# A planned attention and MLP kernel: fillers ahead of the products with v, and the broadcast of inverted sums as a step of its own

## The chip, the cores and the metric

The kernel runs on one core of a Trainium2 chip. A core has TensorE (PE, matrix products), ScalarE (ACT, here the exponentials and tanh), VectorE (DVE, elementwise work), GpSimd (POOL) and SyncE (SP, which issues most of the DMAs). They run side by side and wait for each other through semaphores; each takes its own instructions strictly in order. The metric is the time of one execution in microseconds (us); the time of a kernel is the median of its runs.

## The reference

Two branches are computed from the same x (2048 rows of 640 features) and mixed by a gate:

```
g = sigmoid((x * gate_w).sum(-1))
qkv = x @ wqkv;  32 heads of 20 features
p = softmax(q k^T / sqrt(20));  a = (p v) @ wo
h = x @ w1 + b1  (1536 features)
b = (h * tanh(softplus(h))) @ w2
out = g * a + (1 - g) * b
```

All inputs and the output are bf16. The exponentials of the scores, 32 x 2048 x 2048 of them, are the largest part of the elementwise work.

## The kernel before, in words

**Tiles.** The 32 heads form 8 groups of 4, the 2048 queries form 4 chunks of 512. A score tile is 128 keys by 512 queries of one head; there are 2048 of them. They are kept transposed (keys on the partitions). The first chunks, 0 and 1, are taken group by group, and the projections of q, k and v are made in between; chunks 2 and 3 follow.

**Slots.** The work is cut into 683 slots of three score tiles. In a slot PE makes the three products (`score_mms`, matmul at L1055) into three PSUM banks, ACT takes one exponential over them (L1077, in `emit_e`, PSUM to the buffer ETS, five slots deep), and PE later multiplies the tiles with v (`pv`, L1180), four heads side by side, into one PSUM bank, ACC. v carries a column of ones, so the same product also gives the softmax's sums. Banks 0 to 5 hold the scores of two slots in turn, 6 is ACC, and 7 is for everything else.

**Units.** In some slots the third tile isn't given to ACT: DVE computes its exponential by a polynomial in four operations, and that tile is called a unit. `emit_x` does the first, L1094, which reads the scores from PSUM; the others, L1110 twice and L1112, follow in two lanes. `choose` decides before each slot whether it gets a unit; before it is asked, the loop over slots tests that the work behind its due time is under CATCH_UP, that the lag of tasks is under LAG or little DVE work is queued, and that DVE has room until the end. CHAIN is a reserve in `choose` for the time that a unit needs before its group of heads ends.

**Fillers.** All other matrix work is a list of tasks with due slots: projections (L538, L590, L684, L711), the gate's and the safety test's parts, w1 (`h_task`, L845), w2 (`b_task`, L906) and the output product with wo (L930). A task is some matmuls into bank 7 and a `finish`, which lets DVE drain the bank (for w1 at L855, adding the bias); the next task may begin when the drain is done. `pick` takes the next task that fits into the slot, `put` issues one of its matmuls. What a slot owes to the fillers is counted in `owed`; `now["open"]` is a task that was begun and not ended. A forced task that is due is issued whole, whether it fits or not.

**The plan.** The program is written by a planner that runs when the kernel is built. `Plan.add` appends an instruction to its engine, with assumed costs, and keeps a clock for each engine (`pl.now`); the order in which instructions are added is the order in which each engine takes them. The assumed times only choose the order; on the chip the waits on semaphores decide. `dve` puts an operation on DVE, and before it such queued pieces of DVE work as end within SLACK of the time at which its input is ready (LATER in place of SLACK for drains of fillers when little is owed). `work` picks those pieces from several queues: `norm` first, then the lanes of units, the pieces of the activation (`blend`) and background work.

**Sums.** When a group of heads has had its last product with v, `group_done` copies ACC to OUNG (L1258), and SP moves the sums to RR in a compact form (L1261). The rest stands in the queue `norm`: `invert` takes the reciprocals (L1265), SP writes them to a DRAM buffer SUMS (L1266) and reads them back broadcast over the partitions into BCT (L1268, 256 KB), and `times` multiplies (L1226). OUNG and BCT are held until then. SP adds L1266 and L1268 one right after the other.

**w1 blocks.** `load_w1` (L801, on SP, 320 KB each) loads 48 blocks in turn into two buffers. A block is loaded when the matmuls of the task that used the same buffer have read it; `h_task`'s `finish` adds the load. Their home is the tile W2R for the first 12, then REG.

Of the kernel before, what the change touches and what calls it, by code (L numbers as in the profile page):

```python
# [45 lines left out]
HOP = 0.1  # L46
TAIL = {"pe": 0.17, "act": 0.12, "dve": 0.125, "pool": 0.1, "sp": 2.0}
SWITCH = 0.1
COL = 1 / 2400.0
PASS = CW * COL  # L50
EXP = 1.335
# [3 lines left out]
WIDE = 0.60  # L55
# [2 lines left out]
LANES = 2  # L58
TAKEN = 3.3
SLACK = 0.3  # L60
LATER = 0.9
FREE = 0.2
RISK = {"pe": 0.1, "act": 0.3, "dve": 0.5, "pool": 1.2, "sp": 0.6}
CHAIN = 3.0
AHEAD = 14
BEHIND = 7.0
PATIENCE = 3.0
CATCH_UP = 4.0
BUSY = 0.6
CROWD = 1.4  # L70
MARGIN = 0.5
# [4 lines left out]
LAST = 0  # L76
END = 45
SHIFT = 0.4
LAG = 12
SPARE = 3.5  # L80
WINDOW = 3.41
CALM = 4
# [5 lines left out]
H_AT = 150  # L88
H_STEP = 12.5
THIN = 0.09  # L90
CUTS = ((0, 256), (256, 256))


# [122 lines left out]
def bass_gated_mix__softmax_full_mha__dense_activation_mish__prompt_kernel(  # L216
# [42 lines left out]
    RR = sb("RR", [P, 16], FP32)  # L259
# [12 lines left out]
    SUMS = nc.dram_tensor("SUMS", [HG, CW], FP32, kind="Internal")  # L272
# [54 lines left out]
    NSLOT = -(-NC * NG * NKT * HG // SLOT)  # L327
# [5 lines left out]
    def attention(pl, fast):  # L333
# [4 lines left out]
        tasks = []  # L338
# [3 lines left out]
        norm = deque()  # L342
# [113 lines left out]
        if fast:  # L456
# [328 lines left out]
                return Task([mm(f) for f in range(NFT)], w * COL, finish, due,  # L785
                            lambda: [*sq_ops[n], m_one] if len(sq_ops.get(n, ())) == NFT else None)

            w1_load, w1_last = {}, {}
            w2_load = []

            def load_w1(n):

                k = n % 6
                if n < 2:
                    deps = []
                elif n in (FIRST, FIRST + 1):
                    assert len(sq_ops) >= 4
                    deps = list(wkv_read)
                else:
                    deps = [w1_last[n - 2]]  # L800
                w1_load[n] = pl.add("sp", lambda e: e.dma_start(  # L801
                    w1b(n), B_w1[:, k * HW:(k + 1) * HW].rearrange("(f p) c -> p f c", p=P)),
                    deps, f"w1{n % 2}", cost=0.75, tail=1.7, bulk=1.5)

            def load_w2():
                w2_load.append(pl.add("sp", lambda e: e.dma_start(
# [403 lines left out]
        oung_free, rr_read, bc_read = [None], [None], [None]  # L1210
# [3 lines left out]
        def group_done(c, g, step, last):  # L1214


            end = c == NC - 1 and g >= NG - 1

            def reads():
                if fast:  # L1220
                    return [low_last[0]] if c >= 2 else [zeros, *turned, *(k_moved if g >= 6 else ())]
                assert c < 2 or g > 0 or len(otn_read[c % 2]) == 8
                return otn_read[c % 2]

            def times(src, deps):
                oung_free[0] = bc_read[0] = otn_done[(c, g)] = pl.add("dve", lambda e: e.tensor_tensor(  # L1226
                    otn(c, g, fast), src, BC, ALU.mult), [*deps, *reads()], cost=WIDE)
                if g == NG - 1:
                    otn_read[c % 2] = []

            if end:
                while norm:
                    norm.popleft()[1]()
                if (c, g) == groups[-1]:
                    flush(lambda: not any(soon))
                for at, w in ([cut[(c, g)]] if fast else [(n * HW, HW) for n in range(2)]):
                    cols = slice(at, at + w)
                    src, bc, rr = PS[:, ACC, cols], BC[:, cols], RR[:, at // 32:(at + w) // 32]
                    cost = w * COL * 2.6 + 0.09
                    if (c, g) != groups[-1]:  # L1240
                        held = OUNG[:, cols]
                        last = acc_free[0] = pl.add(
                            "dve", lambda e, src=src: e.tensor_copy(held, src), [last, oung_free[0]], cost=cost)
                        src = held
                    a = pl.add("dve", lambda e, src=src, bc=bc: e.transpose(bc, src), [last, bc_read[0]], cost=cost)
                    a = pl.add("dve", lambda e, bc=bc, rr=rr, w=w: e.reciprocal(rr, bc[:, 0:w:32]), [a, rr_read[0]], cost=0.15)
                    a = pl.add("dve", lambda e, bc=bc, rr=rr, w=w: e.transpose(
                        bc.rearrange("p (a r) -> p a r", r=32), rr.unsqueeze(2).to_broadcast([P, w // 32, 32])),
                        [a], cost=cost)
                    to = otn(c, NG - 1, fast)[:, cols]  # L1250
                    end_done.append(pl.add("dve", lambda e, src=src, bc=bc, to=to: e.tensor_tensor(
                        to, src, bc, ALU.mult), [a, *reads()], cost=cost))
                oung_free[0] = bc_read[0] = rr_read[0] = otn_done[(c, g)] = end_done[-1]
                return
            while oung_free[0] == "busy":
                norm.popleft()[1]()
            src = OUNG[:, :]
            ev = dve(lambda e: e.tensor_copy(src, PS[:, ACC, :]), [last, oung_free[0]], WIDE)  # L1258
            oung_free[0] = "busy"
            acc_free[0] = ev  # L1260
            got = pl.add("sp", lambda e: e.dma_start(  # L1261
                RR[:, :], OUNG[0:P:32, :].rearrange("j (r a) -> j r a", a=16)), [ev, rr_read[0]], "nr0", cost=0.55, tail=1.4)

            def invert():
                r = pl.add("dve", lambda e: e.reciprocal(RR[:, :], RR[:, :]), [got], cost=0.25)  # L1265
                rr_read[0] = pl.add("sp", lambda e: e.dma_start(  # L1266
                    SUMS.ap().rearrange("j (r a) -> (j r) a", a=16), RR[:, :]), [r, *spread_last], "nr1", cost=0.4, tail=1.7)
                spread_last[:] = [pl.add("sp", lambda e: e.dma_start(  # L1268
                    BC, SUMS.ap().unsqueeze(1).to_broadcast([HG, 32, CW])),
                    [rr_read[0], bc_read[0]], "nr2", cost=0.55, tail=4.7)]  # L1270
                spread = list(spread_last)
                norm.append((WIDE, lambda: times(src, spread), lambda: spread[-1]))
            norm.append((0.25, invert, lambda: got))


# [179 lines left out]
        for step in range(NSLOT + 40):  # L1455
            now["step"] = step
            if step >= NSLOT and not queue and not tasks and not any(k >= step for k in at):
                break

            for t in [t for t in tasks if t.forced and t.due <= step]:  # L1460
                while now["open"] not in (None, t):
                    put(now["open"])
                while t in tasks:
                    put(t)
            if step < NSLOT:
                emit_e(step)
            if fast and area[0] and not w2_load and len(h_done) >= FIRST and all(ei_free[(0, b)] != "busy" for b in range(3)):
                load_w2()
            if fast and step == SQ - 18:
                squares(0)  # L1470
                squares(1)
            if acts and safe(acts[0][0]) < pl.now["act"] and mish_free():
                acts.popleft()[1]()
            ahead = able = 0.0
            rate = behind = 0.0
            lag = max((step - t.due for t in tasks if not t.forced and t.ready() is None), default=0)
            for t in tasks:
                slack = max(1, t.due - AHEAD * t.forced - step)
                ahead += t.left()
                rate = max(rate, ahead / slack)  # L1480
                if t.forced or t is now["open"] or t.ready() is not None:
                    able += t.left()
                    behind = max(behind, able / slack)
            now["rate"] = rate
            if step + 2 < NSLOT:
                compose(step + 2, choose(step + 2) if fast and step >= CALM and (step < slot_of(0, 1, 0) or behind < CATCH_UP and (lag < LAG or backlog() < SPARE) and room()) else None)
                emit_s(step + 2)
                to_come = pv_ready() * PASS
                if owed + rate > 0.1 and pick(pl.now["pe"] + 0.8):
                    to_come += min(owed + rate, 0.4)  # L1490
                fill_up(to_come, False)

                if fast and step + 2 in off:
                    emit_x(step + 2)
            emit_pv(step, 2 if step < NSLOT - 1 else 99)

            limit = pl.now["act"] + EXP + HOP if step < NSLOT else 1e9
            owed = min(owed + rate, 1.0) if step < NSLOT else 1e9
            while owed > 0:
                t = pick(limit)  # L1500
                if t is None:
                    break
                put(t)
                owed -= t.cost
            fill_up(0.0, True)
            for fn in at.pop(step, []):
                fn()
            work(pl.now["act"] + 0.5 if step < NSLOT else 1e9)
# [168 lines left out]
```

## Time and profile before

| | |
|---|---|
| median of 3 runs | 880.14 us (878.48 to 881.72) |
| profiled execution | 881.69 us, span 879.9 us |
| busy | ACT 858.4 us (98%), DVE 818.7 (93%), PE 744.8 (85%), POOL 15.4 (2%) |
| exponentials (L1077) | 683, of which 203 over two tiles |
| DMA | 42.44 MB, 48 GB/s over the span |

The span goes from the first to the last instruction; the time of an execution includes a little around it. In rows of groups, the numbers are the line, engine and operation, what is written and read, the count, then the busy time in us and the mean duration of one in ns, then the idle time of that engine just ahead of these instructions and what ended it. A row of waits reads "who <- for whom: us in total, times, longest". A row of the chain is a start, a length and what carried the chain then; a row of the record in order of time is a start, a length, engine, line and operation, with the idle time ahead of it in brackets. SPq rows are DMA issues of SP. A row of stretches is from:to, length, busy time with the count of instructions, the granted clock of TensorE, the share of the DMA engines and GB/s.

### The profile page before, as it was taken

How to read it: one execution, taken by the hardware profiler on the slowest of the kernel's cores; microseconds unless marked ns; L12 is line 12 of the kernel's file. 1: busy time of each engine (PE TensorE's matmuls, PEld its weight loads, DVE VectorE, ACT ScalarE, POOL GpSimd, SP SyncE). 2: the span in 40 equal slices, each digit the busy share in tenths (PEclk: the TensorE clock that was granted, in tenths of full speed). 3: DMA queues.
4: the chain of work that ended last, by engine and by line, in shares of the span. 5: the costliest groups of instructions: out<-in, count | busy, mean ns of one | idle time of the engine just before them, and what ended most of it. 6: DMA issues, size and time to landing. Idle time of an engine off the chain costs nothing.

```text
span 879.9 us, 15312 instructions
## 1 busy us (share of the span) xinstructions
PE 744.8 (85%) x6249; PEld 259.3 (29%) x6291; DVE 818.7 (93%) x1421; ACT 858.4 (98%) x714; POOL 15.4 (2%) x29
## 2 busy tenths in 40 slices
PE   8888888888878888888888888898888788998885
PEld 3232232222322233223223233333333233332222
DVE  5899999999588998999999999999999799999996
ACT  6999999999999999999999999999999799999996
POOL 2000000000000000000000000000000000000000
PEclk9999999999999999999999999999999899999999
DMA  9112110011122110131121121111211212010001
GB/s 215 28 50 60 56 32 13 8 49 37 41 60 63 57 57 28 44 100 37 41 64 42 54 74 31 46 32 40 69 48 43 72 34 71 21 32 18 14 14 35
DMA packets 69870, 42.44 MB, mean 48 GB/s; under 512 B 20472, under 2 KB 65776, under 8 KB 69744
## 3 DMA queue, kind: packets, MB, share of 16 engines
q1 hardware_dynamic: 67424, 40.89, 16.5%
q8 instruction: 52, 0.85, 0.4%
q10 hardware_dynamic: 2256, 0.47, 0.3%
q0 software_dynamic: 112, 0.01, 0.1%
q14 instruction: 26, 0.21, 0.1%
HBM read 33.97 MB, written 5.23 MB: 45 GB/s over the span
## 4 chain that ended last, share of the span: by engine, by line
ACT 95%; PE 2%; DMA 1%; DVE 1%; issue 0%; ACTq 0%
ACT ETS L1077 93%; ACT REG L877 2%; DMA REG<-in_B_w_dram 1%; ACT W2R L877 1%; PE PS L1055 1%; PE PS L490 1%; PE PS L845 0%; DVE HB L936 0%; PE PS L1436 0%; PE PS L649 0%; PE PS L658 0%; PE PS L1180 0%; PE PS L769 0%; PE PS L930 0%; DVE HB L855 0%
## 5 line engine op out<-in xcount | busy, mean ns | idle before, releaser
L1077 ACT ACTIVATE ETS<-PS 128x1536 bf16<-128x1536 f32 (+1 forms) x683 | 837.9, 1479 | 6.2 <-PE PS L1055 6.1
L1055 PE MATMUL PS<-QT,KT 32*128 32x512 bf16 (+1 forms) x2267 | 281.7, 379 | 114.7 <-ACT ETS L1077 102.9
L1180 PE MATMUL PS<-ETS,V_all 128*21 128x512 bf16 (+1 forms) x1901 | 211.5, 380 | 0.3 <-ACT ETS L1077 0.3
L1055 PEld LDWEIGHTS PS<-QT,KT 32*128 32x128 bf16 x2267 | 69.3, 91 | 324.9 <-ACT ETS L1077 302.6
L1180 PEld LDWEIGHTS PS<-ETS,V_all 128*21 128x21 bf16 x1901 | 48.6, 89 | 93.4 <-issue 89.1
L906 PE MATMUL PS<-W2R,HB 128*128 128x320 bf16 x384 | 71.6, 302 | 0.9 <-DVE OUTT L936 0.6
L1110 DVE SCALAR_TENSOR_TENSOR EM<-EM 128x512 f32<-128x512 f32 x101 | 68.9, 682 | 0.1
L1110 DVE SCALAR_TENSOR_TENSOR ER<-ER 128x512 f32<-128x512 f32 x101 | 68.7, 680 | 0.0
L1094 DVE TENSOR_SCALAR XE<-PS 128x512 f32<-128x512 f32 x80 | 54.7, 686 | 8.3 <-PE PS L1055 7.2
L845 PE MATMUL PS<-XB,REG 128*128 128x256 bf16 x360 | 55.2, 279 | 3.7 <-DMA REG<-in_B_w_dram 3.4
L1094 DVE TENSOR_SCALAR REG<-PS 128x512 f32<-128x512 f32 x74 | 50.7, 686 | 2.2 <-PE PS L1055 1.8
L538 PE MATMUL PS<-XB,WOQ 128*128 128x512 bf16 x135 | 42.2, 384 | 2.7 <-issue 2.4
L906 PEld LDWEIGHTS PS<-W2R,HB 128*128 128x128 bf16 x384 | 30.0, 97 | 36.7 <-issue 24.4
L855 DVE TENSOR_TENSOR HB<-PS,B1F 128x512 bf16<-128x512 f32 x48 | 32.9, 685 | 6.0 <-PE PS L845 5.8
L845 PEld LDWEIGHTS PS<-XB,REG 128*128 128x128 bf16 x360 | 29.9, 98 | 28.7 <-issue 22.3
L1094 DVE TENSOR_SCALAR W2R<-PS 128x512 f32<-128x512 f32 x48 | 32.9, 686 | 3.1 <-PE PS L1055 2.4
L896 DVE SCALAR_TENSOR_TENSOR U<-U,HB 128x512 f32<-128x512 f32 x48 | 32.8, 683 | 0.0
L895 DVE SCALAR_TENSOR_TENSOR U<-U 128x512 f32<-128x512 f32 x48 | 32.7, 680 | 0.0
L550 DVE CAST QT<-PS 128x512 bf16<-128x512 f32 x31 | 21.3, 687 | 7.2 <-PE PS L538 6.8
L1110 DVE SCALAR_TENSOR_TENSOR ER<-XE 128x512 f32<-128x512 uint16 x40 | 27.4, 685 | 0.2
L1110 DVE SCALAR_TENSOR_TENSOR EM<-XE 128x512 f32<-128x512 uint16 x40 | 27.3, 683 | 0.2
L1112 DVE SCALAR_TENSOR_TENSOR XE<-ER,XE 128x512 int32<-128x512 f32 x40 | 27.4, 684 | 0.1
(115 smaller groups left out, 797.3 us busy)
## 6 DMA issues: line engine op xcount, KB each, us to landing
REG<-in_B_w_dram SPq DMA_DIRECT2D x36, 320.0 KB, 3.2
BCT<-SUMS SPq DMA_DIRECT2D x31, 256.0 KB
W2R<-in_B_w_dram SPq DMA_DIRECT2D x12, 320.0 KB, 3.2
KT<-KS SPq DMA_DIRECT2D x28, 128.0 KB
KS<-OTN SPq DMA_DIRECT2D x16, 128.0 KB, 1.8
W2R<-in_B_w_dram SPq DMA_DIRECT2D x1, 1920.0 KB, 9.4
out_dram<-OUTT SPq DMA_DIRECT2D x24, 80.0 KB, 1.6
REG<-in_A_wqkv_dram SPq DMA_DIRECT2D x2, 700.0 KB, 8.2
```

What stands on the lines that cost most here:

```text
L538: return lambda e, bank: e.matmul(PS[:, bank, :], pads[:, b, f, :], xt(c)[:, f, :], start=(f == 0), stop=(f == NFT - 1))
L845: return lambda e, bank: e.matmul(PS[:, bank, i * HW:(i + 1) * HW], w1b(n1)[:, f, i * P:(i + 1) * P], xt(c)[:, f, cols], start=(f == 0), s ...
L855: ev = dve(lambda e: e.tensor_tensor(hb, PS[:, bank, :].rearrange("p (i t) -> p i t", i=2), bias, ALU.add), [last, *b1f, *sq_read.values() ...
L895: piece(WIDE, lambda e: e.scalar_tensor_tensor(U2[:, :], U2[:, :], EVEN[0], U2[:, :], ALU.add, ALU.mult))
L896: piece(WIDE, lambda e, to=to: e.scalar_tensor_tensor(U2[:, :], U2[:, :], EVEN[1], to, ALU.add, ALU.mult))
L906: return lambda e, bank: e.matmul(PS[:, bank, 0:HALF], HB[:, hc % 2, f, t * P:(t + 1) * P], W2[:, f, half * HALF:(half + 1) * HALF], start ...
L1055: op = pl.add("pe", lambda e, i=i, g=real(g), tile=tile, j=j, cols=cols, c=c, of_q=of_q: e.matmul(scores(s)[:, i, cols], KT[32 * j:32 * j ...
L1077: e_op[s] = pl.add("act", lambda e: e.activation(ETS[:, s % NETS, 0:n, :], scores(s)[:, 0:n, :], AF.Exp, scale=SCALE, bias=LIFT if fast el ...
L1094: ev_op[s] = dve(lambda e: e.tensor_scalar(y, scores(s)[:, 2, :], SCALE * ULPS, BIAS, ALU.mult, ALU.add), [s_op[s], ei_free[b], *(wkv_read ...
L1110: piece(WIDE, lambda e, v=m if i else f, i=i: e.scalar_tensor_tensor(m, v, STEPS[i], v, ALU.add, ALU.mult), lambda i=i: () if i else [lane ...
L1112: piece(WIDE, lambda e: e.scalar_tensor_tensor(x, m, LAST_STEP, y, ALU.mult, ALU.add))
L1180: lasts[n] = pl.add("pe", lambda e, tile=tile, h=real(g) * HG + j, j=j, src=src[:, cols], of_q=of_q, count=count: e.matmul(PS[32 * j:32 * ...
```

## The change

Four things change, beside parameters of the planner.

In a slot, the rest of a task that is open is issued ahead of the products with v if all of it is at most what is owed plus OVER (0.2 us), and fits before the slot's end with one pass and one switch to spare. Before, fillers came after the products with v in each slot. `emit_pv` itself is not changed.

The spreading of inverted sums, L1268, leaves `invert` and becomes a function `spread`, which is put into the queue `norm` and is taken when the planner holds the write of SUMS to be done. That write is assumed to land 2.8 us after its issue instead of 1.7.

A w1 load also depends on the load before it into the same buffer.

The parameters: LATER 0.9 to 0.5, CHAIN 3.0 to 3.3, CATCH_UP 4.0 to 5.0, LAG 12 to 9. With all of it the plan has 207 units.

```diff
-LATER = 0.9
+LATER = 0.5
-CHAIN = 3.0
+CHAIN = 3.3
-CATCH_UP = 4.0
+CATCH_UP = 5.0
-LAG = 12
+LAG = 9
+OVER = 0.2
...
-            w1_load, w1_last = {}, {}
+            w1_load, w1_last, w1_newest = {}, {}, {}
...
+                deps = [*deps, w1_newest.get(n % 2)]
                 w1_load[n] = pl.add("sp", lambda e: e.dma_start(
                     w1b(n), B_w1[:, k * HW:(k + 1) * HW].rearrange("(f p) c -> p f c", p=P)),
                     deps, f"w1{n % 2}", cost=0.75, tail=1.7, bulk=1.5)
+                w1_newest[n % 2] = w1_load[n]
...
                 rr_read[0] = pl.add("sp", lambda e: e.dma_start(
-                    SUMS.ap().rearrange("j (r a) -> (j r) a", a=16), RR[:, :]), [r, *spread_last], "nr1", cost=0.4, tail=1.7)
+                    SUMS.ap().rearrange("j (r a) -> (j r) a", a=16), RR[:, :]), [r, *spread_last], "nr1", cost=0.4, tail=2.8)
+                norm.append((0.0, spread, lambda: rr_read[0]))
+
+            def spread():
                 spread_last[:] = [pl.add("sp", lambda e: e.dma_start(
                     BC, SUMS.ap().unsqueeze(1).to_broadcast([HG, 32, CW])),
                     [rr_read[0], bc_read[0]], "nr2", cost=0.55, tail=4.7)]
-                spread = list(spread_last)
-                norm.append((WIDE, lambda: times(src, spread), lambda: spread[-1]))
+                wide = list(spread_last)
+                norm.append((WIDE, lambda: times(src, wide), lambda: wide[-1]))
...
-            emit_pv(step, 2 if step < NSLOT - 1 else 99)
-
             limit = pl.now["act"] + EXP + HOP if step < NSLOT else 1e9
             owed = min(owed + rate, 1.0) if step < NSLOT else 1e9
+            if fast and step < NSLOT and now["open"] and now["open"].left() <= min(owed + OVER, limit - pl.now["pe"] - PASS - SWITCH):
+                t = now["open"]
+                while t in tasks:
+                    put(t)
+                    owed -= t.cost
+            emit_pv(step, 2 if step < NSLOT - 1 else 99)
+
             while owed > 0:
```

## The prediction

> **What bounds the kernel now.** I read the page of the profile first: the span, the busy shares and the chain that ended last.
>
> ```profile
> span 879.9 us, 15312 instructions
> PE 744.8 (85%) x6249; PEld 259.3 (29%) x6291; DVE 818.7 (93%) x1421; ACT 858.4 (98%) x714; POOL 15.4 (2%) x29
> ACT 95%; PE 2%; DMA 1%; DVE 1%; issue 0%; ACTq 0%
> ```
>
> ScalarE (ACT) is busy 98% of the span and carries 95% of the chain, so the time is the sum of ACT's exponentials, plus the places where ACT stands idle, plus a start and an end. Second view: ACT's groups by line and shape, and what ACT waited for.
>
> ```profile
> L1077 ACT ACTIVATE ETS<-PS 128x1536 bf16<-128x1536 f32 x480 | 682.4, 1601 | 5.4 <-PE PS L1055 5.4
> L1077 ACT ACTIVATE ETS<-PS 128x1024 bf16<-128x1024 f32 x203 | 225.9, 1191 | 0.8 <-PE PS L1055 0.6
> ACT ETS L1077 <- PE PS L1055: 6.1, 5, 3.8
> ```
>
> A slot is one exponential of three score tiles (480 times) or of two (203 times); in the latter the third tile is a unit that VectorE (DVE) computes. The last slot has two tiles anyway, since 2048 tiles are 682 slots of three and one of two, so 202 units run now. Between first and last exponential ACT waited 6.1 us in five places, 3.8 us of it in one. Third view, the chain at that place (a transfer on it), and the record in order of time around it:
>
> ```profile
> 686.49 7.22 DMA REG<-in_B_w_dram
> ```
>
> ```profile
> 684.42 0.50 PE L845 MATMUL PS<-XB,REG 128*128 128x256 bf16 x3
> ...
> 682.71 0.34 SPq L1266 DMA_DIRECT2D SUMS<-RR  x1
> 685.92 0.53 SPq L1268 DMA_DIRECT2D BCT<-SUMS  x1
> 686.49 11.17 SPq L801 DMA_DIRECT2D REG<-in_B_w_dram  x3
> ...
> 688.45 0.69 DVE L855 TENSOR_TENSOR HB<-PS,B1F 128x512 bf16<-128x512 f32 x1
> ...
> 693.76 1.25 PE L845 MATMUL PS<-XB,REG 128*128 128x256 bf16 x5 [3.42 <-DMA REG<-in_B_w_dram]
> ...
> 695.59 1.45 ACT L1077 ACTIVATE ETS<-PS 128x1536 bf16<-128x1536 f32 x1 [3.76 <-PE PS L1055]
> ...
> 697.85 2.36 ACT L1077 ACTIVATE ETS<-PS 128x1536 bf16<-128x1536 f32 x2 [0.81 <-PE PS L1055]
> ```
>
> SyncE (SP) issues DMAs strictly in order. The w1 block that the task of 693.76 needs could go out when TensorE (PE) had read the buffer two tasks earlier, at 684.42 + 0.50 = 684.92. But ahead of it stood the broadcast L1268, which waited until 685.92 for the write L1266 to land; the load left at 686.49, landed 7.22 us later, PE stood 3.42 us, and ACT lost 3.76 + 0.81 = 4.57 us.
>
> **The change, part by part.**
>
> *Five more units.* 207 units against 202: five exponentials go from three tiles to two, each 1601 - 1191 = 410 ns shorter, so 5 x 0.41 = 2.05 us off the path (if ACT stays the bound). Each adds four vector operations of 128x512 (L1094, two of L1110, L1112):
>
> ```profile
> 207.29 0.68 DVE L1226 TENSOR_TENSOR OTN<-OUNG,BCT 128x512 bf16<-128x512 f32 x1
> 207.89 0.69 DVE L895 SCALAR_TENSOR_TENSOR U<-U 128x512 f32<-128x512 f32 x1
> ```
>
> ```profile
> 200.00:300.00 100.00, 81.72 (x141) 1.00 0.18 55
> 400.00:680.00 280.00, 277.94 (x475) 1.00 0.17 48
> 680.00:700.00 20.00, 15.14 (x26) 0.83 0.33 81
> 700.00:860.00 160.00, 157.60 (x271) 0.99 0.10 28
> ```
>
> The duration is 0.68 us but starts follow each other at 0.60 us, so a unit costs 4 x 0.60 = 2.40 us and five cost 12.0 us of DVE. The four rows below them are DVE's busy time by stage (stretch, its length, busy time). From 200 to 300 us DVE is idle 100 - 81.72 = 18.3 us, which covers 12.0; from 400 on it is idle 2.06 + 2.40 = 4.5 us outside the stall, which does not. The parameter raised, CATCH_UP, is the limit on work that is behind its due time above which no unit is taken; that is early, while projections and the first w1 tasks are owed. I put the units there and cost them nothing on DVE; without that cover they cost up to 12.0 - 4.5 = 7.5 us. Packing products with v for five units differently is at most five more passes of PE; PE's wait for ACT is far above that (below).
>
> *The broadcast as a step of its own.* Now L1266 and L1268 are put into SP's order together; after, L1268 (one DMA of 256 KB, 0.53 us of SP) enters later, when the plan takes the write to have landed, 2.8 us after its issue instead of 1.7. It is moved past whatever SP gets in between: w1 loads (L801), stores (L942), K moves (L568, L582) and loads of wo; POOL's queue is not passed. What SP lost by standing in front of L1268, and the spread of landings:
>
> ```profile
> SPq L1268 <- DMA SUMS<-RR: 51.1, 31, 3.8
> DMA to landing us min/median/max: 3.0/3.2/7.2
> ...
> 603.24 0.53 SPq L1268 DMA_DIRECT2D BCT<-SUMS  x1
> 603.81 0.48 SPq L801 DMA_DIRECT2D REG<-in_B_w_dram  x1
> REG<-in_B_w_dram SPq DMA_DIRECT2D x1, 320.0 KB, 5.8
> ```
>
> SP's 51.1 us of standing cost the path only at 686. (The second row is for L801; the last three show another load right behind a broadcast: 5.8 us to land, hidden there.) With the load ahead it leaves at about 685.0. Best end: it lands in the median 3.2 us, at 688.2, before its PSUM bank is drained (688.45 + 0.69 = 689.14), PE does not stand, and all 4.57 us come back. Worst end: it shares the transfer engines and still takes 7.2, landing at 692.2, which is 1.5 us sooner than 693.71; then about 1.5 comes back. A loss from this load is excluded, since it only moves forward. I take 4.57: the slow landings shown, 5.8 and 7.2, are behind a broadcast, the one ahead of none is the median.
> The Trainium skill, "DMA: Bandwidth & Descriptors", section "Queues, rings and completion order", says that on each transfer engine the descriptors of one issuing queue are consumed in ring order. By that rule a load ahead of the broadcast doesn't share with it, and the sum is that of the best end; sharing would give the worst end. The two slow rows agree with it, but no row here shows the reverse order with both in flight. It also speaks against the change: the broadcast would then land behind 320 KB of w1.
>
> What waits for the later broadcast is L1226 on DVE, and behind L1226 everything of DVE; the sums' buffer OUNG is held until then. In the trace:
>
> ```profile
> 822.74 0.68 DVE L1258 COPY OUNG<-PS 128x512 f32<-128x512 f32 x1
> ...
> 847.59 0.69 DVE L1258 COPY OUNG<-PS 128x512 f32<-128x512 f32 x1
> ...
> 860.00 0.68 DVE L1226 TENSOR_TENSOR QT<-OUNG,BCT 128x512 bf16<-128x512 f32 x1
> SPq L801 <- PE PS L845: 107.8, 22, 16.1
> PE PS L1055 <- ACT ETS L1077: 102.9, 249, 1.2
> ```
>
> Groups follow at 847.59 - 822.74 = 24.9 us and the chain takes 860.00 - 847.59 = 12.4, so 12.5 us are to spare: I cost the delay at nothing. It stops being free if SP stands longer than that.
>
> *The rest of a filler ahead of products with v.* The instructions are the same; the bank of the fillers is drained earlier in the slot, and a pass with v starts later by at most 0.2 us of credit plus what is owed. Its cover is PE's 102.9 us of waiting for ACT (last row above). Zero, between a gain of the other small waits (6.1 - 4.57 = 1.5 us) and a loss of the same size.
>
> *Added dependency of w1 loads, and LATER, CHAIN, LAG.* A w1 load now also waits for the previous load into the same buffer; L801 already waits for matmuls that read that block, so it is never the last. SP's queue behind it doesn't move. The three parameters only choose where units and drains go; they are in the count of 207.
>
> **Sum**, against the profiled execution's 881.69 us: 881.69 - 2.05 - 4.57 = 875.07. That execution lies 1.55 us above the median of 880.14. A stall of DMA timing is the part likeliest to vary between executions, and without it I take profile and median to be alike: 875.1 us, 0.6% down. A difference under 0.5% (4.4 us) is about what a measurement of this kernel can't tell from no change.
>
> **The rivals.**
> 1. *A w1 load is late again.* Every order after the first new unit shifts, and another load can fall behind a broadcast (the two quoted did, one showed). Only the units remain: 880.14 - 2.05 = 878.1. For it: nothing in the change keeps a load from being planned right after a broadcast. Against: none of them stands any more behind the wait for the write. Chance 0.32.
> 2. *Slower: the broadcast is caught behind a long wait of SP.* L801 waited up to 16.1 us for PE. A broadcast put behind such an entry is late by more than the 12.5 us to spare, and DVE stands 16.1 - 12.5 = 3.6 us in front of L1226, with the drains and PSUM banks of units behind it; ACT follows. One such case leaves a gain; from the second on (875.07 + 7.2 = 882.3) it is slower than before; three give 885.9. For it: the step is now free to fall behind other entries. Against: the plan counts SP's waits. Chance 0.12.
> 3. *The units land after 400 us.* DVE becomes the bound there: the stage from 400 to 860 holds 277.94 + 15.14 + 157.60 = 450.7 us of DVE work in 460; 12.0 more is 462.7, so 2.7 over, and 881.69 + 2.7 - 1.55 = 882.8. Against: CATCH_UP bites early. Chance 0.06.
>
> **How the numbers follow.** My forecast has 0.50 (its own range 872.5 to 877, from the small waits of 1.5 us either way, rounded outward); rivals 0.32, 0.12, 0.06. Faster by over 0.5% means under 875.7: three quarters of the forecast's chance and a little of rival 1, 0.41; slower, over 884.5, is rival 2 and a tail of rival 3, 0.13; the rest, 0.46, lies between. The range goes from 872.0 (the fastest run shown, 878.48, less 2.05 and 4.57 is 871.9) to 884.0, which takes in rivals 1 and 3 and leaves out about 0.1 above and 0.07 below.
>
> **What would show it.** Two-tile exponentials 208, three-tile 475. DVE's idle time in 200 to 300 us falls by about 12; from 400 on it stays. SP's wait of L1268 for L1266 falls from 51.1 us to a few, the last broadcast standing behind other SP entries. PE's wait of L845 for a w1 DMA, and ACT's 3.76 us, are gone. I am wrong if L801's longest landing stays near 7 and ACT still waits over 4 us in one place; if DVE waits for BCT in front of L1226 by several us; or if the new units sit after 400 us.

## The result and the profile after

The changed kernel takes 874.3 us (median of four runs, 873.27 to 874.40) against 880.27 us for the kernel before in the same comparison: a ratio of 0.993 with a 95% interval of 0.9915 to 0.9945, 6.0 us or 0.7% down. The forecast was 875.1 us. The profiled execution took 874.34 us, against 881.69 before.

The page after, and ACT's groups and wait for scores (L1080 was L1077 before, L1058 was L1055):

```profile
span 871.9 us, 15314 instructions
PE 753.4 (86%) x6244; PEld 258.2 (30%) x6293; DVE 831.2 (95%) x1441; ACT 855.7 (98%) x714; POOL 15.7 (2%) x29
ACT 95%; PE 2%; DMA 1%; DVE 1%; SPq 0%; issue 0%; ACTq 0%
```

```profile
L1080 ACT ACTIVATE ETS<-PS 128x1536 bf16<-128x1536 f32 x475 | 679.1, 1626 | 0.8 <-PE PS L1058 0.7
L1080 ACT ACTIVATE ETS<-PS 128x1024 bf16<-128x1024 f32 x208 | 233.2, 1215 | 0.0
ACT ETS L1080 <- PE PS L1058: 0.7, 2, 0.5
```

ACT is still what the time consists of. Its exponentials are 475 and 208, as 207 units ask; its waits for scores fell from 6.1 us to 0.7. Between the two profiled spans 8.0 us went: 5.4 us of those waits and 2.05 us for five shorter exponentials make 7.5 of it.

VectorE's busy time by stage, with the same columns as before:

```profile
200.00:300.00 100.00, 96.75 (x170) 1.00 0.21 64
400.00:860.00 460.00, 451.95 (x771) 1.00 0.15 42
```

From 200 to 300 us DVE was idle for 18.3 us; now for 3.3. From 400 to 860 us it is idle for 8.1, against 9.3 with the stall. The five more units are spread out: by the starts of their first operation (L1094 before, L1097 after) one more lies ahead of 200 us, three more from 200 to 300, three more from 300 to 400, and two fewer after 400. Three units are 7.2 us of DVE, so about half of the idle time that went from 200 to 300 us was filled by other work of DVE that moved there. SP's wait and the landings of w1 loads after:

```profile
SPq L1274 <- DMA SUMS<-RR: 22.1, 19, 2.0
DMA to landing us min/median/max: 2.9/3.2/6.5
```

SP still stands in front of the broadcast in 19 of 31 groups, 22.1 us instead of 51.1. The slowest landing, 6.5 us, is of a load at 81.7 us with no broadcast in the 10 us ahead of it; nothing waits for it.

### The profile page after: what moved, and what is told of

It reads as the page before. It is cut to its first block, busy times and chain, and to the rows that moved or that the text cites. A ratio compares the mean times of both kernels' runs of the same rounds, so it can differ in the third digit from the quotient of the medians.

```text
span 871.9 us, 15314 instructions
## 1 busy us (share of the span) xinstructions
PE 753.4 (86%) x6244; PEld 258.2 (30%) x6293; DVE 831.2 (95%) x1441; ACT 855.7 (98%) x714; POOL 15.7 (2%) x29
## 4 chain that ended last, share of the span: by engine, by line
ACT 95%; PE 2%; DMA 1%; DVE 1%; SPq 0%; issue 0%; ACTq 0%
ACT ETS L1080 92%; ACT REG L880 2%; DMA BCT<-SUMS 1%; DMA OTN<-in_A_x_dram 1%; ACT W2R L880 1%; PE PS L1058 1%; PE PS L1183 0%; PE PS L539 0%; PE PS L909 0%; PE PS L659 0%; DVE HB L939 0%; DVE XE L1097 0%; PE PS L650 0%; SPq L583 0%; PE PS L1442 0%
## 5 line engine op out<-in xcount | busy, mean ns | idle before, releaser
L1080 ACT ACTIVATE ETS<-PS 128x1536 bf16<-128x1536 f32 (+1 forms) x683 | 836.6, 1501 | 0.8 <-PE PS L1058 0.7
L1058 PE MATMUL PS<-QT,KT 32*128 32x512 bf16 (+1 forms) x2191 | 275.9, 377 | 99.4 <-ACT ETS L1080 85.5
L1058 PEld LDWEIGHTS PS<-QT,KT 32*128 32x128 bf16 x2191 | 68.3, 91 | 316.1 <-ACT ETS L1080 294.6
L1113 DVE SCALAR_TENSOR_TENSOR EM<-EM 128x512 f32<-128x512 f32 x104 | 70.7, 679 | 0.1
L1097 DVE TENSOR_SCALAR XE<-PS 128x512 f32<-128x512 f32 x82 | 56.1, 684 | 3.2 <-PE PS L1058 1.9
L1097 DVE TENSOR_SCALAR REG<-PS 128x512 f32<-128x512 f32 x76 | 52.1, 686 | 4.0 <-PE PS L1058 2.6
L1097 DVE TENSOR_SCALAR W2R<-PS 128x512 f32<-128x512 f32 x49 | 33.4, 682 | 3.4 <-PE PS L1058 2.9
L848 PEld LDWEIGHTS PS<-XB,REG 128*128 128x128 bf16 x360 | 27.8, 97 | 26.8 <-issue 24.8
L1442 PE MATMUL PS<-KT 128*128 128x512 bf16 x100 | 30.2, 383 | 1.6 <-issue 1.3
```

The lines of the kernel that those rows point to most:

```text
L848: return lambda e, bank: e.matmul(PS[:, bank, i * HW:(i + 1) * HW], w1b(n1)[:, f, i * P:(i + 1) * P], xt(c)[:, f, cols], start=(f == 0), s ...
L1058: op = pl.add("pe", lambda e, i=i, g=real(g), tile=tile, j=j, cols=cols, c=c, of_q=of_q: e.matmul(scores(s)[:, i, cols], KT[32 * j:32 * j ...
L1080: e_op[s] = pl.add("act", lambda e: e.activation(ETS[:, s % NETS, 0:n, :], scores(s)[:, 0:n, :], AF.Exp, scale=SCALE, bias=LIFT if fast el ...
L1097: ev_op[s] = dve(lambda e: e.tensor_scalar(y, scores(s)[:, 2, :], SCALE * ULPS, BIAS, ALU.mult, ALU.add), [s_op[s], ei_free[b], *(wkv_read ...
L1113: piece(WIDE, lambda e, v=m if i else f, i=i: e.scalar_tensor_tensor(m, v, STEPS[i], v, ALU.add, ALU.mult), lambda i=i: () if i else [lane ...
L1442: pl.add("pe", lambda e: e.matmul(PS[:, bank, :], k[:, 0:P], k, start=True, stop=True), [free], cost=PASS, kind="S")
```

## The experiments

Each was compared with runs of the kernel before on the same chip; the median of those was 879.7 to 880.1 us. Ratios are to these.

**One DMA moved.** After planning, the instruction list of the kernel before gets one change, which touches SP's order alone:

```diff
+    b = [o for o in fast.ops if o.slot == "nr2"][24]
+    n = fast.ops.index(b)
+    load = next(o for o in fast.ops[n:] if o.slot in ("w10", "w11"))
+    fast.ops.remove(b)
+    fast.ops.insert(fast.ops.index(load) + 1, b)
```

> The kernel before with one DMA moved in SP's order and nothing else: the 25th broadcast L1268 (685.92 us) goes behind the w1 load that followed it. Theory, the load stood behind the broadcast's wait for the write: TensorE's wait of 3.42 us and ScalarE's 4.57 us vanish, ScalarE's waits for scores fall from 6.1 us to about 1.5, and the time falls by about 4.6 us, to 875.7. Rival, the two transfers share the engines in either order: the load lands about 1.5 us sooner and the time falls by 1.5, to 878.8. Second rival, the stall is there only in some executions: the median moves by less than the profile.

Measured: 876.7 us, ratio 0.9971 (0.9961 to 0.9982), so 1.6 to 3.4 us down; the profiled execution took 877.48 us, 4.2 less than the first one's. SP's record in order of time at that place, the landing of the moved-up load, and ACT's wait:

```profile
683.17 0.34 SPq L1266 DMA_DIRECT2D SUMS<-RR  x1
685.42 0.37 SPq L801 DMA_DIRECT2D REG<-in_B_w_dram  x1
686.13 0.53 SPq L1268 DMA_DIRECT2D BCT<-SUMS  x1
REG<-in_B_w_dram SPq DMA_DIRECT2D x1, 320.0 KB, 3.1
ACT ETS L1077 <- PE PS L1055: 1.8, 5, 0.6
```

The load left 0.71 us ahead of the broadcast and landed in 3.1 us instead of 7.2; TensorE's long wait is gone, and ACT's waits fell by 4.3 us. The order of two DMAs is shown as the cause of that stall. Two things changed with it: the load left without the wait for the write (685.42 instead of 686.49 us), and it went ahead of the broadcast; the landing, 4.1 us shorter, is the larger part.

In the kernel before, ACT lost 4.57 us where TensorE stood only 3.42. Two more rows from there show what was added: behind the stand TensorE's granted clock was 0.50 for 6.8 us, and five matmuls of L845 took 1.25 us (at 693.76), where five had taken 0.72.

```profile
687.69 0.72 PE L845 MATMUL PS<-XB,REG 128*128 128x256 bf16 x5
692.70:699.50 6.80, 5.43 (x29) 0.50 0.17 50
```

The median fell by less than the profile: the executions of the kernel before differ (877.2 to 884.3 us on that chip), and the one first profiled was among the longer ones. Their mean granted clocks differ with them: on another of the chips those with 0.998 took 877.1 to 878.0 us, those with 0.992 took 879.8 to 881.7; the profiled one had 0.993. It may be that the faster ones lack this stall; since only one was profiled, that is not shown.

**SP's order put back in the changed kernel.** Here the changed kernel's list gets each broadcast back behind its write; all other engines keep their order:

```diff
+    for b in [o for o in fast.ops if o.slot == "nr2"]:
+        w = next(d for d in b.deps if d.slot == "nr1")
+        fast.ops.remove(b)
+        fast.ops.insert(fast.ops.index(w) + 1, b)
```

> The changed kernel with only SP's order put back: each of the 31 broadcasts directly behind its write, the order on all other engines and all units as in the changed kernel. If SP's order as such is worth the gain, w1 loads stand behind the write's wait again and up to 4.6 us come back: 876 to 879, with ScalarE's waits for scores back at several us and SP's wait of the broadcast for the write back near 51 us. If the changed order on TensorE and VectorE is what removed the stall, the time stays at 874.3 within 1 us although SP waits 50 us.

Measured: 882.17 us, ratio 1.0029 (1.0018 to 1.0039): more than put back, 7.9 us over the changed kernel and slower than the kernel before. The chain of waits, SP's record, TensorE's waits for DMAs and ACT's wait for scores:

```profile
361.78 13.80 DMA W2R<-in_B_w_dram
630.89 2.47 DMA SUMS<-RR
633.95 7.34 DMA REG<-in_B_w_dram
...
361.20 0.53 SPq L1274 DMA_DIRECT2D BCT<-SUMS  x1
361.78 0.48 SPq L809 DMA_DIRECT2D W2R<-in_B_w_dram  x1
...
PE PS L848 <- DMA REG<-in_B_w_dram: 4.1, 1, 4.1
PE PS L909 <- DMA W2R<-in_B_w_dram: 2.8, 1, 2.8
ACT ETS L1080 <- PE PS L1058: 9.0, 5, 4.3
```

SP's wait for the write is back at 43.8 us. Of the loads that now leave right behind a broadcast, two keep TensorE waiting, the one of w2 (1920 KB) and one of w1. In the changed kernel itself the w2 load goes ahead of the same broadcast:

```profile
360.78 0.37 SPq L809 DMA_DIRECT2D W2R<-in_B_w_dram  x1
361.68 0.53 SPq L1274 DMA_DIRECT2D BCT<-SUMS  x1
W2R<-in_B_w_dram SPq DMA_DIRECT2D x1, 1920.0 KB, 7.9
```

7.9 us ahead, 13.8 behind. In this plan the gain hangs on SP's order; ACT's waits grew by 8.3 us, from 0.7 to 9.0, which covers the 7.9.

**The filler rule alone**, put into the kernel before.

```diff
+OVER = 0.2
...
-            emit_pv(step, 2 if step < NSLOT - 1 else 99)
-
             limit = pl.now["act"] + EXP + HOP if step < NSLOT else 1e9
             owed = min(owed + rate, 1.0) if step < NSLOT else 1e9
+            if fast and step < NSLOT and now["open"] and now["open"].left() <= min(owed + OVER, limit - pl.now["pe"] - PASS - SWITCH):
...
+            emit_pv(step, 2 if step < NSLOT - 1 else 99)
```

> The kernel before with only the rest of a filler put ahead of the products with v (OVER = 0.2); step and parameters as before. The plan then has 209 units, seven more than before, without a higher CATCH_UP. My prediction cost this part at nothing, which would leave 880.3. If the units come from this part and are worth 0.41 us each, 880.3 - 7 x 0.41 = 877.4 with the stall of 4.6 us still somewhere, 872.8 without it. VectorE's idle time from 200 to 300 us falls from 18.3 us by some 15 if they are put there.

Measured: 876.81 us, ratio 0.9966 (0.9952 to 0.998). ACT's wait for scores, and DVE from 200 to 300 us:

```profile
ACT ETS L1078 <- PE PS L1056: 3.2, 6, 1.4
200.00:300.00 100.00, 96.92 (x163) 1.00 0.20 61
```

The part that the prediction cost at nothing brings 3 us by itself, and the idle stage of DVE is filled (3.1 us left) with step and parameters as before. The time is near the 877.4 us that was expected with the stall, but the stall isn't there: ACT's longest wait is 1.4 us. Seven units and 2.9 us less waiting would make 5.8 us; the profiled execution is 4.1 us shorter and the median 2.9, so part of it was lost again, and where is not shown. DVE's waits for products of fillers, before and, in the second fence, with the rule alone:

```profile
DVE QT L550 <- PE PS L538: 6.8, 7, 2.6
DVE V_all L721 <- PE PS L711: 5.9, 4, 2.7
DVE HB L855 <- PE PS L845: 5.8, 5, 3.0
DVE OTN L598 <- PE PS L590: 3.6, 5, 2.3
```

```profile
DVE HB L856 <- PE PS L846: 1.9, 3, 1.2
DVE QT L551 <- PE PS L539: 1.3, 3, 0.9
DVE V_all L722 <- PE PS L712: 0.9, 2, 0.5
DVE OTN L599 <- PE PS L591: 0.2, 1, 0.2
```

22.1 us of standing became 4.3 (3.3 in the changed kernel). DVE had stood waiting for the end of a filler; a task whose rest goes first ends earlier, and seven more units find room. That the tests in front of `choose` are what had refused them is read from the code, not measured. The rule is not the only way to this end: the same four rows add up to 13.7 us with the parameters alone, 9.0 with the step alone, and 6.1 in the next run, which lacks only the rule.

**The changed kernel without the filler rule** (the diff above reversed, the rest kept).

> The changed kernel with the filler rule alone taken out (the step, the parameters and the w1 dependency kept); 206 units. If the filler rule carries the change, the time goes back most of the way: 878 to 880, although there are four units more than before (1.6 us); ScalarE's waits for scores or its other idle time then have to be larger. If the units alone decide, 874.3 + 0.4 = 874.7.

Measured: 878.87 us, ratio 0.9995 (0.9984 to 1.0005): no gain clear of noise is left, although the plan has 206 units and DVE is idle for only 7.2 us from 200 to 300. So neither the units nor the filled idle time make the gain alone. ACT's record over its exponentials, before, here, and in the changed kernel, ends with the start of the last one:

```profile
L1077 ACT ACTIVATE ETS<-PS x683: 1017/1507/1847, 10.2 to 869.7; 128x1536 bf16<-128x1536 f32 x120, 128x1024 bf16<-128x1024 f32 x51
```

```profile
L1079 ACT ACTIVATE ETS<-PS x683: 1006/1494/1840, 10.1 to 864.1; 128x1536 bf16<-128x1536 f32 x118, 128x1024 bf16<-128x1024 f32 x53
```

```profile
L1080 ACT ACTIVATE ETS<-PS x683: 1018/1538/1885, 10.5 to 861.9; 128x1536 bf16<-128x1536 f32 x120, 128x1024 bf16<-128x1024 f32 x51
```

Without the rule ACT came to its last slot 5.6 us sooner than before, but its span is 877.2 us: 13.1 us follow, against 879.9 - 869.7 = 10.2 before and 871.9 - 861.9 = 10.0 in the changed kernel. About 3 us were given back behind the last exponential. ACT's last operation waits there for the output product with wo, a filler; here and in the changed kernel:

```profile
ACT EM L1547 <- PE PS L932: 5.2, 1, 5.2
ACT EM L1553 <- PE PS L933: 2.5, 1, 2.5
```

Fillers were left over: behind the start of the last exponential DVE still drains seven output products (L938), in the changed kernel four (L939), in the kernel before five. Of the 5.3 us between this span and that of the changed kernel, 3.1 lie in this end. The other 2.2 lie ahead of it: one unit less is 0.4, ACT's waits for scores (1.5 us against 0.7) are 0.8, and the rest is open.

**The changed kernel without the step** (L1268 added with its write when the plan is made, as before; 1.7 us assumed).

> The changed kernel with the broadcast added right behind its write when the plan is made, as before (filler rule, parameters and w1 dependency kept); 206 units. If the step of its own is what takes away the stall of a w1 load: 874.3 + 0.4 + up to 4.6 = 875 to 879, with ScalarE waiting several us for scores. If the filler rule takes it away: 874.7 within 1 us.

Measured: 874.95 us, ratio 0.995 (0.9936 to 0.9964), with 1.0 us of ACT waiting for scores. So the step is worth 0.65 us in the change by the medians, (0.995 - 0.993) x 880 = 1.8 us by the ratios, at the edge of what these runs separate. It doesn't contradict the 7.9 us above. Here too the w2 load leaves right behind a broadcast and takes as long:

```profile
362.07 0.53 SPq L1271 DMA_DIRECT2D BCT<-SUMS  x1
362.64 0.48 SPq L809 DMA_DIRECT2D W2R<-in_B_w_dram  x1
W2R<-in_B_w_dram SPq DMA_DIRECT2D x1, 1920.0 KB, 13.6
```

But no row of TensorE's waits names a DMA. A load behind a broadcast is slow, and costs nothing where the plan needs it late enough. That the planner, which counts SP's standing when it puts broadcast and write together, orders the rest accordingly is read from the code; when only SP's order is changed afterwards, nothing else makes way.

**The step alone**, in the kernel before.

> The kernel before with only the broadcast as a step of its own (and the write taken to land after 2.8 us); 204 units. If the step as such is what helps: two units are worth 0.8 us, and with the stall of a w1 load gone (as in the run with one DMA moved) 879.7 - 0.8 - 3.0 = 875.9. If it is worth little when the plan is made anew: 878.9 within 1.5 us.

Measured: 880.0 us, ratio 1.0004 (0.9995 to 1.0013). The stall of 3.8 us went, but other waits took its place, 4.7 us in all, among them a kind that wasn't there:

```profile
ACT ETS L1077 <- PE PS L1055: 2.9, 6, 0.6
ACT ETS L1077 <- PE PS L1180: 1.8, 2, 1.0
```

**The parameters alone**, in the kernel before (LATER 0.5, CHAIN 3.3, CATCH_UP 5.0, LAG 9).

> The kernel before with only LATER 0.5, CHAIN 3.3, CATCH_UP 5.0 and LAG 9; 203 units. If the raised CATCH_UP is what puts units into VectorE's idle time, as my prediction had it, that idle time from 200 to 300 us falls from 18.3 us by some 10 and the time falls; with one unit more in all I now expect it to stay: 879.3 within 1.5 us, with the stall of a w1 load there or not, by chance of the order.

Measured: 878.04 us, ratio 0.9988 (0.9976 to 1.0). DVE's idle time from 200 to 300 us fell from 18.3 to 7.3 us; there are only 203 units. The stall of a w1 load is not in this trace either: ACT waits 2.1 us for scores in all, at most 0.6 at once.

```profile
200.00:300.00 100.00, 92.69 (x152) 1.00 0.18 55
```

**CATCH_UP back at 4.0** in the changed kernel.

```diff
-CATCH_UP = 5.0
+CATCH_UP = 4.0
```

> The changed kernel with CATCH_UP back at 4.0; 207 units as with 5.0. If CATCH_UP opens the early stage to units, as my prediction had it, VectorE's idle time from 200 to 300 us rises from 3.3 us to 10 or more. If the filler rule does it, idle time stays and the time is 874.3 within 0.7 us.

Measured: 873.66 us, ratio 0.9934 (0.9921 to 0.9948), the same as the changed kernel; DVE's idle time from 200 to 300 us is 3.3 us, the same too.

```profile
200.00:300.00 100.00, 96.73 (x169) 1.00 0.21 64
```

**OVER at 0** in the changed kernel.

```diff
-OVER = 0.2
+OVER = 0.0
```

> The changed kernel with OVER at 0: the rest of a filler goes first only within what the slot owes, with no credit; 207 units. If going ahead of the products with v is what counts, the time stays at 874.3 within 1 us. If the credit of 0.2 us is needed to end tasks in time, 876 or more.

Measured: 875.64 us, ratio 0.9949 (0.9936 to 0.9963), 1.3 us over the changed kernel by the medians, between the two expectations. ACT's waits for scores are 2.5 us instead of 0.7. Going ahead is most of the rule (without it the time was 878.87 us); the credit's share is at the edge of what these runs separate.

**Fewer units** in the changed kernel.

```diff
-compose(step + 2, choose(step + 2) if fast and step >= CALM and
+compose(step + 2, choose(step + 2) if fast and len(off) < 0.29 * (step + 2) and step >= CALM and
```

> The changed kernel with a cap on units: a slot is only offered one while fewer than 0.29 times the slots so far have one, which leaves 196 units, spread over the whole run. If a unit is worth 0.41 us, as the two exponentials differ: 874.3 + 11 x 0.41 = 878.8. If VectorE with 207 units already holds up other engines, fewer units cost less than that: 874.3 to 877.

Measured: 878.14 us, ratio 0.9981 (0.9972 to 0.999). Eleven units fewer cost 3.8 us by the medians, 0.35 us each, or (0.9981 - 0.993) x 880 = 4.5 us, 0.41 each, by the ratios. ACT's waits are 1.0 us, so it is the units that are missing, and nothing here shows that DVE with 207 of them holds up the rest.

**Late broadcasts** in the changed kernel: the slower rival, made to happen in three groups.

```diff
+    for k in (15, 17, 19):
+        b = [o for o in fast.ops if o.slot == "nr2"][k]
+        user = next(o for o in fast.ops if b in o.deps and o.eng == "dve")
+        fast.ops.remove(b)
+        n = fast.ops.index(user)
+        b.deps.append(next(o for o in reversed(fast.ops[:n]) if o.eng == "pe"))
+        fast.ops.insert(n, b)
```

> The changed kernel with three of the 31 broadcasts (the 16th, 18th and 20th) issued late: each goes in SP's order to just ahead of the multiplication L1229 that needs it, and waits there for the TensorE instruction that precedes that place. This is the second rival of the prediction (a broadcast caught behind a long wait), made to happen. VectorE then stands about 5 us in front of L1229, three times. If ScalarE follows one to one, as the rival priced it, the time rises by about 15 us, to 889. If the slots already made cover part of it, by 3 x 2 to 3 us, to 880 to 883. If it is hidden, under 1 us.

Measured: 900.04 us, ratio 1.0238 (1.0219 to 1.0256), 25.7 us over the changed kernel, far beyond the expectation. The record in order of time around the first of the three, and who waited in total:

```profile
449.11 0.53 SPq L1274 DMA_DIRECT2D BCT<-SUMS  x1
...
454.64 0.69 DVE L1229 TENSOR_TENSOR OTN<-OUNG,BCT 128x512 bf16<-128x512 f32 x1 [7.96 <-DMA BCT<-SUMS]
...
459.08 0.80 PE L848 MATMUL PS<-XB,REG 128*128 128x256 bf16 x3 [7.83 <-DVE HB L858]
...
460.47 1.02 ACT L1080 ACTIVATE ETS<-PS 128x1024 bf16<-128x1024 f32 x1 [7.92 <-PE PS L1058]
...
DVE QT L1229 <- DMA BCT<-SUMS: 14.4, 2, 7.4
DVE OTN L1229 <- DMA BCT<-SUMS: 9.2, 2, 8.0
```

DVE stood for 7.96 us, and TensorE for 7.83 and ACT for 7.92 behind it: there is no slack between them. The broadcast takes 5.5 us from issue to use here. DVE's 23.6 us in front of L1229 are nearly all of the 25.7, and ACT's waits, 20.1 us for scores and 5.4 us for L901 of DVE, are as long. The same group in the changed kernel, whose record agrees with this one up to there and where DVE didn't wait:

```profile
438.50 0.52 SPq L1274 DMA_DIRECT2D BCT<-SUMS  x1
446.59 0.68 DVE L1229 TENSOR_TENSOR OTN<-OUNG,BCT 128x512 bf16<-128x512 f32 x1
```

The broadcast left 449.11 - 438.50 = 10.6 us later, and DVE stood for 7.96 of them. So only 2.6 us were to spare.

## Why the prediction was right, and where it was not

*What bounds the kernel, and the sum.* Right: 875.1 predicted, 874.3 measured, within both ranges given. In the profiled executions, which the sum was made against, 881.69 - 874.34 = 7.35 us went where 6.62 were predicted. The medians differ by 6.0. Alone, the filler rule brings 3.0 us, the parameters 1.1 and the step nothing, by the ratios. What is missing to 6 is either the parts working together or the added dependency of w1 loads, which the prediction put at nothing and which no run takes out or adds alone.

*Five units for 2.05 us.* Right in size: the run with fewer units prices one at 0.35 to 0.41 us. (The count of 207 was known from the plan.) That they cost DVE nothing was right too, but only three of the five went to the stretch from 200 to 300 us.

*"The parameter raised, CATCH_UP"* as what opens that room: wrong. With CATCH_UP back at 4.0 in the changed kernel the number of units, DVE's idle time and the time stay. In the kernel before, the four parameters together do fill that stretch (7.3 us idle), but bring only one unit and 0 to 2 us; which of the four does it was not tried.

*"The rest of a filler ahead of products with v ... Zero"*: the step that failed most. The rule alone gives 209 units and 3 us, and without it no gain clear of noise is left. The prediction looked for its cost on TensorE, where none shows, and not at who waits for the end of a filler: DVE had 22.1 us in the rows of its waits for L538, L711, L845 and L590. Nor did it look at the end of the run, where fillers that are late are left over behind the last exponential: 3.1 us when the rule is taken out of the changed kernel.

*The broadcast as a step, 4.57 us.* The mechanism was right for the stall: one DMA moved takes it away, and a load ahead of a broadcast lands in 3.1 us, the best end. Its size was overstated for the median, 1.6 to 3.4 us measured; the sum took the stall of one longer execution for that of all. And the stall's end was put down to the wrong part of the change: without the step the changed kernel has no such stall either (874.95 us, ACT waiting 1.0 us). The stall belonged to one order, and any new order could lose it or make another, as the step alone and the parameters alone show. That the terms added up to the right time is partly luck: a term too large for the median and a term of nothing that was worth 3 us.

*"12.5 us are to spare"* for the broadcast: a wrong reading. It counts until OUNG is written again, but DVE takes its work in order and stands as soon as it comes to the multiplication; the first of the late broadcasts shows 2.6 us to spare. The delay still cost nothing, since the plan put broadcast and multiplication so that DVE waits for BCT only 0.7 us in all.

*"SP's wait ... falls to a few"*: it fell to 22.1 us; in 19 groups the broadcast still stands at its write.

*Rival 1*, another late load: it didn't come in the changed kernel, but the run with SP's order put back had two that TensorE waited for. *Rival 2*: right that ACT follows DVE one to one, wrong in price, because it subtracts the 12.5 us. With 2.6 us to spare, a broadcast held up for 16.1 us would leave DVE standing for about 13.5, an estimate from these two numbers, and not 3.6. (Nor was 16.1 the longest wait: L801 waited up to 18.3 us for L1055, in another row of the same view.) No such case came in the changed kernel. *Rival 3* is excluded: DVE has 8.1 us idle after 400 us, and two units fewer.

The ring order rule of the Trainium skill, "DMA: Bandwidth & Descriptors", section "Queues, rings and completion order", gave the best end of the broadcast's term; the runs agree: 3.1 us for the load 0.71 us ahead of a broadcast, and 5.6 to 7.3 us for w1 loads 0.57 us behind one.

## What to carry to other kernels

In a program whose order is planned, a part that adds no instruction can be the one that matters: ask which engine waits for the end of each piece that is moved, not only which engine issues it. A stall read from one execution is one order's accident as well as one execution's; undo it by moving a single instruction before counting it as the gain of a rule. Taking a rule out can cost in another place than putting it in gains: here units when it is put in, the end of the run when it is taken out. And put a large load that is needed soon ahead of a slow broadcast on the same queue; one that is needed late can stand behind it.

## What was not expected of the hardware

A transfer's time depended on which of two neighbours left first: the 320 KB load took 3.1 us when issued 0.71 us ahead of the 256 KB broadcast, and such loads took 5.6 to 7.3 us in these runs when issued 0.57 us behind it; the 1920 KB load took 7.9 us when issued 0.90 us ahead, 13.8 and 13.6 us when issued 0.58 and 0.57 us behind. And a stand of 7.96 us on VectorE came out as 7.92 us on ScalarE, by way of TensorE (7.83), which waited for VectorE to drain a bank. TensorE's stand of 3.42 us in the kernel before was followed by 6.8 us at a granted clock of 0.50.
